# Attention backward: transposes of X ahead of the next block's first outputs, small row factors on Pool, one more empty slot in a background chain

## The chip, the cores and the metric

The kernel runs on one core of a Trainium2 chip. A core has TensorE (PE, matmuls), VectorE (DVE), ScalarE (ACT), GpSimd (Pool) and SyncE (SP, used here to issue DMAs). Each works through its own queue in order. The metric is device microseconds of one execution; a time before and a time after are medians over several runs. A profile is one execution, so its times are taken from that execution alone.

## The reference

The reference computes one block (attention of 32 heads with a head size of 16, an MLP with gelu, and a gate) and the gradients of its inputs. Sequence 2048, model size 512, MLP size 1792, all tensors in bf16:

```python
x = A_x
xn = _layernorm(x, axis=-1)
s = _A_ref(xn, A_wqkv, A_wo)            # softmax(q k^T / 4) v, then @ wo
g = _silu(_B_ref(xn, B_w1, B_b1, B_w2, B_b2))   # layernorm, gelu MLP
return x + s * g
```

The outputs are this value and its gradients with respect to A_x, A_wqkv, A_wo, B_w1, B_b1, B_w2 and B_b2 for a given grad_out (`jax.vjp`).

## The kernel before

Three stages follow each other. `phase_pre` makes the layer norms, q, k, v, the MLP's forward values and the gradient that enters the attention, and leaves them in DRAM. `attention_core` computes the attention forward and its gradients of q, k and v in one pass. `phase3` makes the remaining weight and input gradients. The change lies in `attention_core` alone, whose instruction order is written out by hand (`manual_schedule`): the order in which the Python code emits instructions is the order in each engine's queue.

Heads are handled in 16 pairs `p`, the 2048 queries in four chunks `qc` of 512. A pair and a chunk make a block, so there are 64 blocks `j`. A block has 16 steps, one for each key block `kb` of 128 keys; the global step number is `g`, with kb = g % 16. The pass is software-pipelined: while the steps of a block compute its exponentials and products, the Z matmuls of the block before it run three steps late (`lagb = 3`).

In each step:

- PE makes the scores `s` of the next step (`emit_s`, L696), the product `d` of the output gradient and the values for both heads (`emit_d`, L708), and in 10 of 16 steps the scores in the other orientation, `t` (`emit_t`, L682). The other six tiles of that kind come by DMA transpose.
- ACT takes the exponential of `s` into `eg` (`emit_exp_a`, L722) and of `t` into `e` (`emit_exp_b`, L730).
- DVE multiplies `d` by the exponential, once for each head (`emit_mult`, L740).
- PE accumulates X with the matmuls of the step before: `emit_l` (row sums, L766), `emit_e` (L778), `emit_g` (L790). X is one PSUM tile, so the next block's first `emit_l` must wait until X has been copied out.
- PE accumulates Z, the gradients of keys and values, of the block before (`emit_ze`, `emit_zg`, L856 and L868); after every four steps DVE adds Z to `acc` (`emit_acc`, L880 and L882).
- every fourth step SP issues a DMA transpose of `eg` into `tg` (`emit_dmat`, L751).

The scores share two PSUM buffers, and `d` shares two others with the transposed X (`ps_d`, tag "d"): a new `d` needs the product of the `d` before last to be done.

At the end of a block ACT copies X to `xs` (L795). In step 1 of the following block `emit_finalize` turns it into the outputs of 512 queries: four PE transposes of `xs` into XT (L805), a DVE copy to `xt` (L807), the reciprocal of the row sums `rL` (L817), the factors `dl` (L819) and `ndr` (L821), all 128x8. Pool then makes the weights W1 and W2 of the Z matmuls (L811, L822 to L824) and writes the attention output and the gradient of q (L826 to L833). The first Z matmul of a block that needs the new W1 is emitted at the end of step 3. In the order before, `emit_l`, `emit_e` and `emit_g` of step 0 stand ahead of the transposes in PE's queue.

Pool has three other tasks. At the start of a pair's second chunk and later (`load_ops`, `late`) it issues the loads of the next pair (L583 to L585) and copies them into a padded tile (L588, L589, and L596, L597 at step 13). When the last chunk of a pair has been accumulated it adds the two halves of `acc` (`hi`, `ob`, L888 and L889) and issues four DMAs of the result (L894); the last of this falls into steps 2 to 4 of the second chunk of the next pair, where the padding copies at step 5 follow. And a generator, `gelu_slope_ops`, computes the slope of the gelu for 56 tiles in the background. One of its slots is used at the end of each step, except at the steps kb = 2 and 3 and where `emit_finalize` runs (kb = 1), so a block has 13 slots. One iteration takes 12 slots: eleven hold Pool instructions (L631 and L632, loads L621, the store L657), one is empty. One of the slots also puts a Tanh into ACT's queue (L639), whose input `v` Pool makes in the slot before, and whose result Pool uses two slots later.

Of the kernel before, what the change touches and what calls it, by code (L numbers as in the profile page):

```python
# [9 lines left out]
f32 = mybir.dt.float32  # L10
ACT = mybir.ActivationFunctionType
ALU = mybir.AluOpType
# [529 lines left out]
def attention_core(ctx, tc, NAT_s, NATQ_s, Oall, dQall, dKVT_out, ident_f32, H1T_s, GP_s, npairs=16, nqc=4):  # L542
    nc = tc.nc
# [14 lines left out]
    finp = sb("finp", 2)  # L558
# [4 lines left out]
    for i in range(2):  # L563
# [4 lines left out]
            NATQq=opnd.tile([128, 16, 2, 17], bf16, name=f"NATQq{i}"),  # L568
            NATQd=opnd.tile([128, 16, 2, 16], bf16, name=f"NATQd{i}"),
# [34 lines left out]
    blocks = [(p, qc) for p in range(npairs) for qc in range(nqc)]  # L604
    NB = len(blocks)
    NSTEP = NB * 16
    st_s, st_t, st_d, st_et, st_e = {}, {}, {}, {}, {}
    blk = [dict(Gk={}, Ek={}) for _ in range(NB)]
# [8 lines left out]
    def gelu_slope_ops():  # L617
        def load(i):
            sc, fc = divmod(i, FC)
            x = bgp.tile([128, 512], bf16, name="bg_x")  # L620
            nc.gpsimd.dma_start(out=x[:], in_=H1T_s[fc * 128:(fc + 1) * 128, sc * 512:(sc + 1) * 512])  # L621
            return x
        nx = load(0)
        yield
        for i in range(n_slope):
            sc, fc = divmod(i, FC)
            x = nx
            m = bgp.tile([128, 512], bf16, name="bg_m")
            v = bgp.tile([128, 512], f32, name="bg_v", bufs=1)
            t = bgp.tile([128, 512], f32, name="bg_t", bufs=1)  # L630
            ts = lambda out, in_, a, b: nc.gpsimd.tensor_scalar(out=out[:], in0=in_[:], scalar1=a, scalar2=b, op0=ALU.mult, op1=ALU.add)  # L631
            tt = lambda out, a, b, op=ALU.mult: nc.gpsimd.tensor_tensor(out=out[:], in0=a[:], in1=b[:], op=op)  # L632
            tt(m, x, x)
            yield
            ts(v, m, GA, 1.0)
            yield
            tt(v, v, x)
            yield
            nc.scalar.activation(out=t[:], in_=v[:], func=ACT.Tanh, scale=GC)  # L639
            ts(m, m, 1.5 * GA * GC, 0.5 * GC)  # L640
            yield
            tt(m, m, x)
            if i + 1 < n_slope:
                nx = load(i + 1)
            yield
            tt(v, t, t)
            yield
            ts(v, v, -1.0, 1.0)
            yield
            tt(m, m, v)  # L650
            yield
            ts(t, t, 0.5, 0.5)
            yield
            tt(m, m, t, ALU.add)
            yield
            yield
            nc.gpsimd.dma_start(out=GP_s[fc * 128:(fc + 1) * 128, sc * 512:(sc + 1) * 512], in_=m[:])  # L657
            yield
    bg = gelu_slope_ops()

    def a_unit(g):
        return (g // 16, g % 16) if 0 <= g < NSTEP else None
# [5 lines left out]
    def op_of(j):  # L668
        return OP[blocks[j][0] % 2]
# [15 lines left out]
    def emit_s(g):  # L685
        a = a_unit(g)
        if a is None:
            return
        j, kb = a
        op = op_of(j)  # L690
        qc = blocks[j][1]
        s = ps_st.tile([128, 2, 512], f32, name="s", tag="st")
        st_s[g] = s
        for hj in range(2):
            r = 32 * hj
            nc.tensor.matmul(s[:, hj, :], lhsT=op["KVT"][r:r + 32, kb * 128:(kb + 1) * 128], rhs=op["QDT"][r:r + 32, qc * 512:(qc + 1) * 512],  # L696
                             start=True, stop=True, tile_position=(r, 0))
# [27 lines left out]
    def emit_exp_b(g):  # L725
        if g not in st_t:
            return
        e = ep.tile([128, 2, 512], bf16, name="e")
        st_e[g] = e
        nc.scalar.activation(out=e[:], in_=st_t.pop(g)[:], func=ACT.Exp)  # L730
# [12 lines left out]
    def emit_dmat(g):  # L743
        a = a_unit(g)
        if a is None or a[1] % 4 != 3:
            return
        j, kb = a
        kc = kb // 4
        n = n_moved[kc]
        tg = tgp.tile([128, 48, 128], bf16, name="tg")  # L750
        nc.sync.dma_start_transpose(out=tg[:, 0:8 * n + 32, :], in_=st_et[g][0][:, (4 - n) * 1024:8192])  # L751
        for i in range(n):
            blk[j]["Ek"][(kc, 4 - n + i)] = tg[:, 8 * i:8 * i + 8]
        blk[j]["Gk"][kc] = tg[:, 8 * n:8 * n + 32]
# [40 lines left out]
            nc.scalar.copy(out=xs[:], in_=X[:])  # L795
            blk[j]["xs"] = xs

    def emit_finalize(j):
        p, qc = blocks[j]
        NQq = op_of(j)["NATQq"]  # L800
        NQd = op_of(j)["NATQd"]
        xs = blk[j].pop("xs")
        XT = ps_d.tile([128, 4, 128], f32, name="XT", tag="d")
        for qb in range(4):
            nc.tensor.transpose(XT[:, qb, :], xs[:, qb * 128:(qb + 1) * 128], ident_f32[:])  # L805
        xt = finp.tile([128, 4, 128], f32, name="xt", bufs=1)
        nc.vector.tensor_copy(out=xt[:], in_=XT[:])  # L807
        XTv = xt[:].rearrange("q b (r c) -> q b r c", r=4)
        W1 = wp.tile([128, 4, 2, 32], bf16, name="W1")
        W2 = wp.tile([128, 4, 2, 32], bf16, name="W2")  # L810
        nc.gpsimd.memset(W2[:, :, :, 0:16], 0.0)  # L811
        st0 = qc * 4
        nqs = NQq[:, st0:st0 + 4, :, 1:17]
        ndo = NQd[:, st0:st0 + 4, :, :]
        bc = lambda ap: ap.to_broadcast([128, 4, 2, 16])
        rL = finp.tile([128, 4, 2, 1], f32, name="rL")
        nc.vector.reciprocal(out=rL[:], in_=XTv[:, :, 2:4, 17:18])  # L817
        dl = finp.tile([128, 4, 2, 1], f32, name="dl")
        nc.vector.tensor_tensor(out=dl[:], in0=XTv[:, :, 2:4, 0:1], in1=rL[:], op=ALU.mult)  # L819
        ndr = finp.tile([128, 4, 2, 1], f32, name="ndr")  # L820
        nc.vector.scalar_tensor_tensor(out=ndr[:], in0=dl[:], scalar=-1.0, in1=rL[:], op0=ALU.mult, op1=ALU.mult)  # L821
        nc.gpsimd.tensor_tensor(out=W1[:, :, :, 0:16], in0=ndo, in1=bc(rL[:]), op=ALU.mult)  # L822
        nc.gpsimd.tensor_tensor(out=W2[:, :, :, 16:32], in0=nqs, in1=bc(rL[:]), op=ALU.mult)
        nc.gpsimd.tensor_tensor(out=W1[:, :, :, 16:32], in0=nqs, in1=bc(ndr[:]), op=ALU.mult)  # L824
        Ov = Oall[:, st0:st0 + 4, p * 32:(p + 1) * 32].rearrange("q b (h c) -> q b h c", h=2)
        nc.gpsimd.tensor_tensor(out=Ov, in0=XTv[:, :, 0:2, 16:32], in1=bc(rL[:]), op=ALU.mult)  # L826
        t1 = finp.tile([128, 4, 2, 16], f32, name="t1")
        nc.gpsimd.tensor_tensor(out=t1[:], in0=XTv[:, :, 0:2, 0:16], in1=bc(dl[:]), op=ALU.mult)
        nc.gpsimd.tensor_tensor(out=t1[:], in0=XTv[:, :, 2:4, 1:17], in1=t1[:], op=ALU.subtract)
        rL4 = finp.tile([128, 4, 2, 1], f32, name="rL4")  # L830
        nc.gpsimd.tensor_scalar(out=rL4[:], in0=rL[:], scalar1=0.25, scalar2=None, op0=ALU.mult)
        dQv = dQall[:, st0:st0 + 4, p * 32:(p + 1) * 32].rearrange("q b (h c) -> q b h c", h=2)
        nc.gpsimd.tensor_tensor(out=dQv, in0=t1[:], in1=bc(rL4[:]), op=ALU.mult)  # L833
        blk[j]["W1"] = W1
        blk[j]["W2"] = W2
# [67 lines left out]
    for g in range(NSTEP + 16 + lagb):  # L903
        a = a_unit(g)
        if a is not None:
            j, kb = a
            p, qc = blocks[j]
            if kb == 0 and qc == 1 and p + 1 < npairs:
                for i, f in enumerate(load_ops(p + 1)):
                    late.append((g + 1 + 4 * i, f))  # L910
        for it in [x for x in late if x[0] <= g]:
            late.remove(it)
            it[1]()
        first = g % 16 == 1
        gz = g - lagb
        i = gz % 4
        emit_s(g + 1)
        emit_d(g, 0)
        if not first:
            emit_l(g - 1)  # L920
        if i == 0:
            emit_e(g - 1)
        else:
            emit_ze(gz)
            if i % 2 == 1:
                emit_zg(gz - 1)
                emit_zg(gz)
        emit_d(g, 1)
        emit_t(g)
        emit_exp_a(g + 1)  # L930
        emit_exp_b(g)
        emit_mult(g)
        emit_acc(gz)
        emit_dmat(g)
        if first:
            emit_l(g - 1)
        if i != 0:
            emit_e(g - 1)
        emit_g(g - 1)
        if i == 0:  # L940
            emit_ze(gz)
        if g >= 17 and (g - 17) % 16 == 0 and (g - 17) // 16 < NB:
            emit_finalize((g - 17) // 16)
        elif g % 16 not in (2, 3):
            next(bg, None)
    for it in late:
# [108 lines left out]
```

## Time and profile before

| | |
|---|---|
| Median of 4 runs | 2495.18 us (2484.98 to 2521.93) |
| The profiled execution | 2490.88 us |
| Its span, first to last instruction | 2488.9 us |
| Mean granted TensorE clock | 0.951 |
| First and last copy of X (L795) | 328.4 and 2071.6 us |
| PE products of `d` (L708) | 2048, 392 ns each |
| ACT exponentials of `s` (L722) and `t` (L730) | 1024 of 1034 ns, 640 of 1036 ns |
| DVE products (L740) | 2048, 686 ns each |
| DVE waiting for XT at L807 | 60.0 us, 64 times |
| ACT waiting for Pool before the Tanh (L639) | 11.1 us, 4 times |

How to read it: the attention stage takes some 1780 us of the span. A row of the page gives a group's busy time and the mean of one instruction; instructions of one engine overlap a little at their ends, so starts that follow each other are closer than the durations say (exponentials that run back to back start 0.92 us apart). The idle time behind the second bar is that of the engine just before the group, with the engine whose instruction ended it.

### The profile page before, as it was taken

How to read it: one execution, taken by the hardware profiler on the slowest of the kernel's cores; microseconds unless marked ns; L12 is line 12 of the kernel's file. 1: busy time of each engine (PE TensorE's matmuls, PEld its weight loads, DVE VectorE, ACT ScalarE, POOL GpSimd, SP SyncE). 2: the span in 40 equal slices, each digit the busy share in tenths (PEclk: the TensorE clock that was granted, in tenths of full speed). 3: DMA queues.
4: the chain of work that ended last, by engine and by line, in shares of the span. 5: the costliest groups of instructions: out<-in, count | busy, mean ns of one | idle time of the engine just before them, and what ended most of it. 6: DMA issues, size and time to landing. Idle time of an engine off the chain costs nothing.

```text
span 2488.9 us, 47595 instructions
## 1 busy us (share of the span) xinstructions
PE 2231.0 (90%) x18408; PEld 757.4 (30%) x18448; DVE 1843.3 (74%) x3222; ACT 1815.5 (73%) x2102; POOL 1113.3 (45%) x1678
## 2 busy tenths in 40 slices
PE   3688599999999999999999999999999997589997
PEld 2233122222222222222222222222222222234446
DVE  5665388898889888888888988888889883112652
ACT  3354289999899999899898999989999994011241
POOL 0533454666557476665657575664313121110020
PEclk8799689999999999999899999999999998789999
DMA  5355499999999999999999999999999998997565
GB/s 192 99 185 180 110 225 224 251 235 241 218 246 239 237 245 239 229 229 247 222 232 230 235 233 223 254 227 233 224 232 232 231 217 202 260 231 204 150 125 125
DMA packets 1743125, 534.88 MB, mean 215 GB/s; under 512 B 1664433, under 2 KB 1721906, under 8 KB 1742898
## 3 DMA queue, kind: packets, MB, share of 16 engines
q1 hardware_dynamic: 1671554, 449.37, 89.0%
q10 hardware_dynamic: 61104, 54.93, 7.2%
q0 software_dynamic: 10240, 27.54, 3.8%
q8 instruction: 144, 2.36, 0.4%
q14 instruction: 83, 0.68, 0.1%
HBM read 52.83 MB, written 62.66 MB: 46 GB/s over the span
## 4 chain that ended last, share of the span: by engine, by line
PE 51%; ACT 18%; DMA 11%; DVE 8%; POOL 6%; issue 4%; SPq 2%; ACTq 1%; DVEq 0%; POOLq 0%
PE d L708 10%; PE X L766 9%; ACT e L730 8%; PE s L696 8%; ACT eg L722 7%; PE X L778 4%; DMA tg<-eg 4%; PE X L790 3%; PE Z L868 3%; PE ps_dhg L465 2%; DVE eg L740 2%; PE Z L856 2%; DMA hgc<-HGT_s 1%; PE ps_h L212 1%; DMA hgc<-DH1T_s 1%
## 5 line engine op out<-in xcount | busy, mean ns | idle before, releaser
L740 DVE TENSOR_TENSOR eg<-d,eg 128x512 bf16<-128x512 f32 x2048 | 1340.6, 686 | 182.8 <-PE d L708 71.4
L722 ACT ACTIVATE eg<-s 128x1024 bf16<-128x1024 f32 x1024 | 1042.4, 1034 | 96.7 <-PE s L696 43.2
L708 PE MATMUL d<-QDT,KVT 32*128 32x512 bf16 x2048 | 800.9, 392 | 14.3 <-DVE eg L740 14.0
L730 ACT ACTIVATE e<-t 128x1024 bf16<-128x1024 f32 x640 | 663.0, 1036 | 47.9 <-PE t L682 46.1
L696 PE MATMUL s<-QDT,KVT 32*128 32x512 bf16 x2048 | 408.0, 393 | 72.4 <-ACT eg L722 54.2
L766 PE MATMUL X<-eg,Lc 128*32 128x512 bf16 x2048 | 412.0, 399 | 5.3
L778 PE MATMUL X<-eg,NAT 128*32 128x512 bf16 x2048 | 411.7, 399 | 0.0
L790 PE MATMUL X<-eg,NAT 128*17 128x512 bf16 x2048 | 406.0, 393 | 0.0
L708 PEld LDWEIGHTS <-KVT 32*128 32x128 bf16 x2048 | 186.9, 91 | 342.4 <-issue 342.4
L856 PE MATMUL Z<-e,W 128*32 128x512 bf16 x1280 | 255.9, 395 | 4.7 <-POOL W L824 3.8
L682 PE MATMUL t<-KVT,QDT 32*128 32x512 bf16 x1280 | 254.6, 392 | 5.4 <-ACT eg L722 5.2
L822 POOL TENSOR_TENSOR W<-NATQd,rL 128x128 bf16<-128x128 bf16 x64 | 25.8, 402 | 468.6 <-DVE rL L817 468.6
L696 PEld LDWEIGHTS <-KVT 32*128 32x128 bf16 x2048 | 116.0, 91 | 307.1 <-issue 307.0
L868 PE MATMUL Z<-tg,W 128*32 128x512 bf16 x2048 | 208.5, 388 | 0.0
L766 PEld LDWEIGHTS <-Lc 128*32 128x32 bf16 x2048 | 104.4, 93 | 329.0 <-issue 324.9
L856 PE MATMUL Z<-tg,W 128*32 128x512 bf16 x768 | 154.3, 398 | 0.0
L778 PEld LDWEIGHTS <-NAT 128*32 128x32 bf16 x2048 | 99.4, 94 | 165.1 <-issue 165.1
L882 DVE TENSOR_TENSOR acc<-Z,acc 128x512 f32<-128x512 f32 x192 | 130.5, 680 | 13.1 <-PE Z L868 13.1
L856 PEld LDWEIGHTS <-W 128*32 128x32 bf16 x2048 | 113.5, 93 | 38.7 <-issue 24.9
L270 POOL TENSOR_TENSOR dx<-lnb_prod,lnb_dy 128x512 bf16<-128x512 f32 x16 | 20.3, 1266 | 214.0 <-DMA dout<-in_grad_out_dram 184.4
L790 PEld LDWEIGHTS <-NAT 128*17 128x17 bf16 x2048 | 93.5, 88 | 59.5 <-issue 59.5
L632 POOL TENSOR_TENSOR bg_v<-bg_t 128x512 f32<-128x512 f32 x56 | 58.4, 1043 | 80.0 <-ACT bg_t L639 79.3
(167 smaller groups left out, 2729.5 us busy)
## 6 DMA issues: line engine op xcount, KB each, us to landing
HGT_s<-hgT SPq DMA_DIRECT2D x2, 3584.0 KB, 12.4
bg_x<-H1T_s POOLq DMA_DIRECT2D x56, 128.0 KB, 5.4
GP_s<-bg_m POOLq DMA_DIRECT2D x56, 128.0 KB, 5.4
gp<-GP_s ACTq DMA_DIRECT2D x8, 896.0 KB, 6.9
DH1T_s<-dh1T SPq DMA_DIRECT2D x4, 1792.0 KB, 10.3
NAT<-NAT_s POOLq DMA_DIRECT2D x16, 264.0 KB, 6.0
GB_s<-gB ACTq DMA_DIRECT2D x16, 256.0 KB, 2.0
tg<-eg SPq DMA_TRANSPOSE x256, 8.6
```

The lines of the kernel that those rows point to most:

```text
L682: nc.tensor.matmul(t[:, hj, :], lhsT=op["QDT"][r:r + 32, q0:q0 + 128], rhs=op["KVT"][r:r + 32, kc * 512:(kc + 1) * 512], start=True, stop= ...
L696: nc.tensor.matmul(s[:, hj, :], lhsT=op["KVT"][r:r + 32, kb * 128:(kb + 1) * 128], rhs=op["QDT"][r:r + 32, qc * 512:(qc + 1) * 512], start ...
L708: nc.tensor.matmul(d[:], lhsT=op["KVT"][r:r + 32, kb * 128:(kb + 1) * 128], rhs=op["QDT"][r:r + 32, qc * 512:(qc + 1) * 512], start=True, ...
L722: nc.scalar.activation(out=cur["eg"][1][:, :, kb % 4, :, :].rearrange("k b h q -> k h b q"), in_=st_s.pop(g)[:].rearrange("k h (b q) -> k ...
L730: nc.scalar.activation(out=e[:], in_=st_t.pop(g)[:], func=ACT.Exp)
L740: nc.vector.tensor_tensor(out=gts[:, kb % 4, hj, :].rearrange("k (b q) -> k b q", b=4), in0=ds[hj][:].rearrange("k (b q) -> k b q", b=4), ...
L766: nc.tensor.matmul(X[64 + 32 * hj:96 + 32 * hj, :], lhsT=Lc[:], rhs=et[:, :, kb % 4, hj, :], start=(kb == 0), stop=False, skip_group_check ...
L778: nc.tensor.matmul(X[32 * hj:32 * hj + 32, :], lhsT=NATt[:, kb, hj, 1:33], rhs=et[:, :, kb % 4, hj, :], start=(kb == 0), stop=(kb == 15), ...
L790: nc.tensor.matmul(X[64 + 32 * hj:64 + 32 * hj + 17, :], lhsT=NATt[:, kb, hj, 0:17], rhs=gts[:, kb % 4, hj, :], start=False, stop=(kb == 1 ...
L856: nc.tensor.matmul(Z[32 * hj:32 * hj + 32, :], lhsT=blk[j]["W1"][:, qb, hj, :], rhs=ev[:, hj], start=(i == 0), stop=False, tile_position=( ...
L868: nc.tensor.matmul(Z[c:c + 32, :], lhsT=blk[j]["W2"][:, qb, hj, :], rhs=gv[:, :, hj, qb, :], start=(i == 1), stop=(i >= 2), tile_position= ...
L882: nc.vector.tensor_tensor(out=av, in0=Z[:], in1=av, op=ALU.add)
```

## The change

The transposes of X, their copy and the reciprocal move from `emit_finalize` into a new `emit_xt`, which is emitted ahead of `emit_l`, `emit_e` and `emit_g` in the same step. `dl` and `ndr` go from DVE to Pool; `ndr` becomes two Pool instructions, and both halves of W1 now stand ahead of W2. The generator gets one more empty slot between the slot that makes `v` and the one that issues the Tanh, so that an iteration takes 13 slots.

```diff
             tt(v, v, x)
             yield
+            yield
             nc.scalar.activation(out=t[:], in_=v[:], func=ACT.Tanh, scale=GC)
             ts(m, m, 1.5 * GA * GC, 0.5 * GC)
...
-    def emit_finalize(j):
-        p, qc = blocks[j]
-        NQq = op_of(j)["NATQq"]
-        NQd = op_of(j)["NATQd"]
+    def emit_xt(j):
         xs = blk[j].pop("xs")
         XT = ps_d.tile([128, 4, 128], f32, name="XT", tag="d")
         for qb in range(4):
             nc.tensor.transpose(XT[:, qb, :], xs[:, qb * 128:(qb + 1) * 128], ident_f32[:])
         xt = finp.tile([128, 4, 128], f32, name="xt", bufs=1)
         nc.vector.tensor_copy(out=xt[:], in_=XT[:])
+        XTv = xt[:].rearrange("q b (r c) -> q b r c", r=4)
+        rL = finp.tile([128, 4, 2, 1], f32, name="rL")
+        nc.vector.reciprocal(out=rL[:], in_=XTv[:, :, 2:4, 17:18])
+        blk[j]["xt"] = (xt, rL)
+
+    def emit_finalize(j):
+        p, qc = blocks[j]
+        NQq = op_of(j)["NATQq"]
+        NQd = op_of(j)["NATQd"]
+        xt, rL = blk[j].pop("xt")
...
-        rL = finp.tile([128, 4, 2, 1], f32, name="rL")
-        nc.vector.reciprocal(out=rL[:], in_=XTv[:, :, 2:4, 17:18])
+        nc.gpsimd.tensor_tensor(out=W1[:, :, :, 0:16], in0=ndo, in1=bc(rL[:]), op=ALU.mult)
         dl = finp.tile([128, 4, 2, 1], f32, name="dl")
-        nc.vector.tensor_tensor(out=dl[:], in0=XTv[:, :, 2:4, 0:1], in1=rL[:], op=ALU.mult)
+        nc.gpsimd.tensor_tensor(out=dl[:], in0=XTv[:, :, 2:4, 0:1], in1=rL[:], op=ALU.mult)
         ndr = finp.tile([128, 4, 2, 1], f32, name="ndr")
-        nc.vector.scalar_tensor_tensor(out=ndr[:], in0=dl[:], scalar=-1.0, in1=rL[:], op0=ALU.mult, op1=ALU.mult)
-        nc.gpsimd.tensor_tensor(out=W1[:, :, :, 0:16], in0=ndo, in1=bc(rL[:]), op=ALU.mult)
+        nc.gpsimd.tensor_scalar(out=ndr[:], in0=dl[:], scalar1=-1.0, scalar2=None, op0=ALU.mult)
+        nc.gpsimd.tensor_tensor(out=ndr[:], in0=ndr[:], in1=rL[:], op=ALU.mult)
+        nc.gpsimd.tensor_tensor(out=W1[:, :, :, 16:32], in0=nqs, in1=bc(ndr[:]), op=ALU.mult)
         nc.gpsimd.tensor_tensor(out=W2[:, :, :, 16:32], in0=nqs, in1=bc(rL[:]), op=ALU.mult)
-        nc.gpsimd.tensor_tensor(out=W1[:, :, :, 16:32], in0=nqs, in1=bc(ndr[:]), op=ALU.mult)
...
         emit_dmat(g)
+        fin = (g - 17) // 16 if first and 0 <= (g - 17) // 16 < NB else None
+        if fin is not None:
+            emit_xt(fin)
         if first:
             emit_l(g - 1)
...
-        if g >= 17 and (g - 17) % 16 == 0 and (g - 17) // 16 < NB:
-            emit_finalize((g - 17) // 16)
+        if fin is not None:
+            emit_finalize(fin)
```

## The prediction

> **What bounds the kernel now.** I read the page first (busy shares, the clock row), then the busy time of a long stretch of the attention stage, then the order of time around one block change, and last the waits on the tanh. The profiled execution took 2490.88 us with a span of 2488.9 us; the median of the four runs shown is 2495.18 us, 4.3 us above it. All sums below are made against the 2490.88 us.
>
> ```profile
> PE 2231.0 (90%) x18408; PEld 757.4 (30%) x18448; DVE 1843.3 (74%) x3222; ACT 1815.5 (73%) x2102; POOL 1113.3 (45%) x1678
> ...
> PEclk8799689999999999999899999999999998789999
> 332.00:2072.00 1740.00, 1659.58 (x15595) 492.91 (x15593) 1525.39 (x2514) 1610.52 (x1752) 955.35 (x1506) 0.98 1.16 234
> ```
>
> Between 332 and 2072 us PE is busy for 95%, ACT for 93%, DVE for 88%, Pool for 55% of the time. No engine is saturated alone; what counts is which hand-over comes late. 1740 us hold 63 blocks, 27.6 us each. The order of time around one block change (start, duration, engine, line; in brackets the idle time before and what ended it):
>
> ```profile
> 1019.98 0.58 ACT L795 COPY xs<-X 128x512 f32<-128x512 f32 x1
> 1020.61 0.39 PE L766 MATMUL X<-eg,Lc 128*32 128x512 bf16 x2
> 1021.15 0.66 PE L805 MATMUL XT<-ident_f,xs 128*128 128x128 f32 x4
> 1021.91 0.69 DVE L807 COPY xt<-XT 128x512 f32<-128x512 f32 x1 [0.91 <-PE XT L805]
> 1023.27 1.27 DVE L740 TENSOR_TENSOR eg<-d,eg 128x512 bf16<-128x512 f32 x2
> 1024.00 0.37 PE L708 MATMUL d<-QDT,KVT 32*128 32x512 bf16 x1 [0.24 <-DVE eg L740]
> 1025.95 1.02 ACT L722 ACTIVATE eg<-s 128x1024 bf16<-128x1024 f32 x1 [0.80 <-PE s L696]
> ```
>
> X is copied by 1020.56 (I call that base). PE first does the six matmuls of emit_l, emit_e and emit_g, then the transposes; DVE idles 0.91 us for them, copies, makes three small factors, and starts its next product at base+2.71. PE's next d needs the PSUM buffer which that product frees and starts at 1024.00, although its partner s started at 1023.37; elsewhere the two start within 0.01 us. That 0.6 us reaches ACT as 0.80 us of idleness.
>
> The second loss is rare and large:
>
> ```profile
> 996.63 2.02 POOL L894 DMA_DIRECT2D dKVT_s<-ob  x4 [0.29 <-POOL ob L889]
> 998.66 1.16 POOL L632 TENSOR_TENSOR bg_v<-bg_v,bg_x 128x512 f32<-128x512 f32 x1
> ...
> 999.86 0.63 ACT L639 ACTIVATE bg_t<-bg_v 128x512 f32<-128x512 f32 x1 [2.76 <-POOL bg_v L632]
> ...
> 1001.45 0.39 PE L696 MATMUL s<-QDT,KVT 32*128 32x512 bf16 x2 [3.29 <-ACT eg L722]
> ```
>
> ```profile
> 988.54:1020.55 32.01, 28.39 (x248) 7.64 (x248) 24.41 (x41) 26.25 (x30) 23.31 (x38) 0.89 1.10 232
> 1102.17:1129.09 26.92, 25.59 (x248) 7.75 (x248) 24.45 (x41) 25.52 (x29) 21.64 (x36) 1.00 1.25 257
> 1326.51:1359.14 32.63, 29.01 (x250) 7.68 (x248) 24.59 (x40) 26.22 (x29) 22.90 (x37) 0.84 1.11 234
> ```
>
> ACT stands in its queue behind a tanh whose input Pool has not finished, PE runs dry, and its granted clock falls to a mean of 0.84 to 0.89 over the block. The tile bg_t shows four such waits, 11.1 us in all. Each makes a block of 32.0 to 33.0 us from one of 26.9 to 27.2: some 5.5 us.
>
> [...] gaps of 3.29 us and even 1.67 us are followed by half clock here. [...] an instruction that waits holds those behind it, as the tanh above does. [...] 128x8 takes 0.234 us (L831), 128x128 0.40 us.
>
> **The change, part by part.**
>
> *Transposes forward.* They need xs (base) and the buffer of d whose product ended 0.15 us before base, so they can start at base+0.05 instead of 0.59. They hold PE 0.59 us (to the next matmul), so the six matmuls follow at 0.64 and the next s at 1.18, as now: PE's order changes, not its sum. DVE copies from 0.81 to 1.50 (the lag of 0.10 behind the transposes and 0.69 as now). No DMA issue moves with it.
>
> *Two factors leave DVE, the reciprocal stays.* rL ends at 1.73; dl (0.17) and ndr (0.27) no longer follow on DVE. The next product starts at 1.77 instead of 2.71 and ends at 2.46. s of that step must still wait for an exp of ACT and starts at 2.81 as now; its d follows at once instead of at 3.44: 0.62 us won. The next d but one waits for DVE too and comes 0.76 us earlier (DVE's chain moves from 3.31 to 2.55 there, where it meets the d at 2.09). I take 0.65 us, 64 times: -41.6 us. Bounds: 0, if another wait steps in; 0.94 us, all that DVE gains, -60 us.
>
> *Pool's chain.* Before the last W1 half stand now dl, the two steps of ndr, instead of W2. No row shows a 128x8 product on Pool. Low end 0.17 us each (the 128x512 and 128x128 products, 1.1 and 0.40 us, carried down to 8 elements); high end 0.40 us, the 128x128 row. I take 0.25 with hand-over, 0.75 us together. W1 is done at about 1.83 + 0.36 + 0.75 + 0.40 = 3.3; the first Z matmul that needs it comes at base+4.63 now, 4.0 then. Hidden with 0.7 us to spare; if the cover goes, each 0.1 us costs PE 0.1 us. With the high end W1 is done at 3.8, still in time.
>
> *The extra yield.* An iteration of the background slope now takes 13 slots, and a block has 13 (16 steps less 1, 2 and 3). So each iteration sits at the same place of every block, where 12 slots let it drift: v is finished at step 5, the tanh comes after the exps of step 7. In blocks of the first query chunk that follow a finished pair (13 while the background runs) Pool has, in program order: load of the next pair, finalize, hi/ob, four dKVT issues, v's first half, two Pad copies, v's second half. From base: the last slope product before it ends 0.17; three issues 1.7 -> 1.9; finalize 3.2 + 0.75 -> 5.85; hi, ob and issues 4.33 (as from 994.32 to 998.65) -> 10.2; 0.62 -> 10.8; Pad copies 1.2 -> 12.0; product 1.16 and hand-over -> 13.2. ACT has done the exp before the tanh at base+11.3 in the undisturbed block above; 0.65 earlier makes 10.7. So ACT waits 2.5 us in all 13, where it waits 2.76 us in 4 now. Costs scale from 5.5 us: 5.2. Nine more are +47 us, four a little shorter -1 us. Behind the tanh stand the exps, and behind these PE's s and DVE's products. The yield adds no work.
>
> *Other blocks.* After a tanh at this place no block lost time before (26.8 us). Blocks behind a standstill are shorter (27.13 us against 28.56 and 28.60 for two others), since the DMA transposes catch up: for nine more about -6 us after deducting seams that wait for DMA anyway.
>
> Sum: -41.6 + 47 - 1 - 6 = -1.6 us, 2489 us for the profiled execution; between that and the median's offset I say 2490.
>
> **The rivals.**
>
> *A, the standstills vanish.* If v is ready by base+10.7 in the pair blocks, the seams gain 42 us and the four waits' 22 us go: 2491 - 42 - 22 = 2427. For it: a tanh one slot later is exactly more time for Pool. Against: 2.5 us are missing and Pool's list has no gap.
>
> *B, the new Pool chain holds PE up (the slower side).* Place: the first Z matmul of each block, waiting for W1. Price: whatever W1 passes base+4.0 by. It decides from three small operations of 0.47 us each; at 0.7 us each all 0.65 us of a seam are gone. Then only the standstills' +47 - 6 remain: 2532. For it: Pool waited for here already (W, 3.8 us on PE). Against: 0.234 us for the like-sized L831.
>
> *C, the transposes do not come forward.* The profile puts 0.43 us of the wait before them down to DVE; if they need the second product (base+0.44) they hold the six matmuls, DVE gains only its 0.44 us, PE loses that much: seam gain nil, 2532. Against: in the profile they start 0.32 us behind the matmul ahead of them, PE's usual pace, and in some blocks before that product has ended.
>
> **Chances.** Likeliest case 0.66 (its own range 2462 to 2521: 0.4 to 0.9 us per seam, 4.6 to 6.3 us per standstill), A 0.13, B 0.13, C 0.08. The range 2450 to 2536 holds the first and B and C, and leaves A out. Faster by over 1% (below 2470; about what a measurement of this kernel can tell from no change): 0.13 + 0.05 = 0.18. Slower (above 2520): 0.21 of which some falls short, plus the first case's edge: 0.20. Within: 0.62.
>
> **What will show it.** In the profile after: DVE's wait for XT falls from 0.94 to about 0.4 us a block; the d behind s at a block change starts with it; ordinary blocks are 26.2 us. bg_t has 13 waits for Pool of about 2.5 us, 32 us in all, 108 us apart, each followed by half clock. No new wait of Z for W. The prediction is wrong if the waits on bg_t are few or short (then A), if Z waits for W in most blocks (B), or if half clock follows less often than 13 times.

## The result, and the profile after

| | before | after |
|---|---|---|
| Median of all runs | 2503.95 us (61 runs, 2481.78 to 2535.66) | 2525.77 us (38 runs, 2483.64 to 2551.24) |
| Ratio of comparable runs | 1 | 1.0023, interval 1.0000 to 1.0047 |
| The profiled execution | 2490.88 us | 2545.43 us |
| Its span and mean granted clock | 2488.9 us, 0.951 | 2543.7 us, 0.897 |

The change makes the kernel slower by about 0.2%, at the edge of what can be told from nothing. Comparable runs are those within 1.5% of their kernel's fastest; the medians of all runs differ by 0.9%, and the profile after is of a run outside that limit. The forecast was 2490 us against 2495.18 us, so 0.2% faster: the time lies in the range, the sign is wrong. The two profiled executions are 55 us apart, much more than the medians: before's is 13 us better than its median, after's 20 us worse. The granted clock goes with the time of an execution: the fastest of after, 2483.64 us, had a mean of 0.927, the slowest, 2551.24 us, one of 0.898.

From the profile of after, the busy times, the clock row (tenths of full speed, 40 slices) and ACT's row of the exponentials; then the same row of before:

```profile
PE 2289.9 (90%) x18408; PEld 750.1 (29%) x18448; DVE 1830.7 (72%) x3094; ACT 1821.2 (72%) x2102; POOL 1155.0 (45%) x1870
PEclk8799669898989989898898989898998998799998
L723 ACT ACTIVATE eg<-s 128x1024 bf16<-128x1024 f32 x1024 | 1045.2, 1034 | 93.8 <-PE d L709 81.5 <-DMA tg<-eg 5.7 <-DVE eg L741 1.6
L722 ACT ACTIVATE eg<-s 128x1024 bf16<-128x1024 f32 x1024 | 1042.4, 1034 | 96.7 <-PE s L696 43.2 <-PE d L708 36.5 <-DMA tg<-eg 8.5
```

The work is the same, but PE is busy for 59 us longer, since its clock falls again and again. The clock records of all kernels here show two values, full clock (1.0) and half clock (0.5). In the attention stage nearly every second slice is an 8 where before had 9. ACT's wait for `s`, 43.2 us in the profile before, no longer shows in its row; its wait for `d` has grown from 36.5 to 81.5 us.

The order of time around a block change of after (start, duration, engine, line; X has been copied at 534.28):

```profile
533.70 0.58 ACT L796 COPY xs<-X 128x512 f32<-128x512 f32 x1
534.63 0.63 PE L803 MATMUL XT<-ident_f,xs 128*128 128x128 f32 x4 [0.38 <-DVE eg L741]
535.19 0.39 PE L767 MATMUL X<-eg,Lc 128*32 128x512 bf16 x2
535.36 0.69 DVE L805 COPY xt<-XT 128x512 f32<-128x512 f32 x1 [0.28 <-PE XT L803]
535.73 0.39 PE L697 MATMUL s<-QDT,KVT 32*128 32x512 bf16 x2
535.73 0.39 PE L709 MATMUL d<-QDT,KVT 32*128 32x512 bf16 x1
536.16 1.02 ACT L723 ACTIVATE eg<-s 128x1024 bf16<-128x1024 f32 x1
536.26 1.45 DVE L741 TENSOR_TENSOR eg<-d,eg 128x512 bf16<-128x512 f32 x2
```

`s` and `d` start together and ACT no longer idles there: its 0.80 us are won, and a block without trouble takes 25.98 us instead of 26.80. Now the other side: who waited for XT, and for the tanh's input, in all of after (engine that was waited for; us and times):

```profile
  PE XT L803: 26.6, 63
```

```profile
  POOL bg_v L632: 33.0, 13
```

DVE waits 0.42 us a block for XT. The tanh waits 13 times, 33.0 us. All stand in the second block of a pair, called a pair block below. One of them, in the block that begins at 445.8, in order of time:

```profile
453.94 2.04 POOL L901 DMA_DIRECT2D dKVT_s<-ob  x4 [0.29 <-POOL ob L896]
456.06 0.61 POOL L631 TENSOR_SCALAR bg_v<-bg_m 128x512 f32<-128x512 bf16 x1
456.72 0.67 POOL L588 COPY Pad<-NAT 128x544 bf16<-128x544 bf16 x1
457.33 0.60 POOL L589 COPY Pad<-NAT 128x512 bf16<-128x512 bf16 x1
457.91 1.15 POOL L632 TENSOR_TENSOR bg_v<-bg_v,bg_x 128x512 f32<-128x512 f32 x1
459.08 0.63 ACT L640 ACTIVATE bg_t<-bg_v 128x512 f32<-128x512 f32 x1 [2.08 <-POOL bg_v L632]
460.68 0.61 PE L697 MATMUL s<-QDT,KVT 32*128 32x512 bf16 x2 [2.90 <-ACT eg L723]
```

Pool's list ends at base + 13.3, as foretold. The exponential behind the tanh in ACT's queue starts at 459.62, 0.54 us after the tanh, and PE stands for 2.90 us. From then on the matmuls of `s` take 0.61 us instead of 0.39. Busy times of this block, the next and the one after it (window, length, then PE, PEld, DVE, ACT and Pool busy with counts, granted clock, DMA share, GB/s):

```profile
445.80:480.90 35.10, 32.13 (x248) 7.46 (x248) 23.95 (x38) 26.39 (x29) 22.16 (x39) 0.70 1.15 226
480.90:508.30 27.40, 26.96 (x253) 8.00 (x251) 24.53 (x40) 25.71 (x30) 13.97 (x24) 0.95 1.05 226
508.30:534.30 26.00, 25.42 (x248) 7.66 (x248) 23.62 (x38) 25.54 (x30) 13.97 (x24) 1.00 1.05 235
```

A gap of 2.90 us makes a block 9.1 us longer, and the half clock runs into the next block too. In an undisturbed block ACT and PE are busy for 98% of the time: no slack is left to catch up in.

Between copies of X, blocks 2 to 62 take 1689.8 us in the profile before and 1726.2 us after, 36.4 us more. This sum is made up as follows: 61 blocks at 0.82 us less, -50.0 us; what lies above the undisturbed length grows from 55.0 us (before, over 26.80) to 141.4 us (after, over 25.98). Of the 141.4 us, 112.3 are in the 13 blocks with a tanh wait, 7.2 in block 57, 19.1 in the blocks behind these. The other 18 us of the two spans' difference are 11.8 us in the first block, which ran at half clock throughout, and the rest outside.

### The profile page after: what moved, and what is told of

It is laid out like the page before. It is cut to its first block, busy times and chain, and to the rows that moved or that the text cites. A ratio compares the mean times of both kernels' runs of the same rounds, so it can differ in the third digit from the quotient of the medians.

```text
span 2543.7 us, 47712 instructions
## 1 busy us (share of the span) xinstructions
PE 2289.9 (90%) x18408; PEld 750.1 (29%) x18448; DVE 1830.7 (72%) x3094; ACT 1821.2 (72%) x2102; POOL 1155.0 (45%) x1870
## 4 chain that ended last, share of the span: by engine, by line
PE 53%; ACT 17%; POOL 10%; DMA 9%; DVE 5%; issue 4%; SPq 1%; ACTq 1%; POOLq 0%; DVEq 0%
PE d L709 10%; PE s L697 10%; PE X L767 10%; ACT eg L723 8%; ACT e L731 7%; PE X L779 6%; PE Z L875 3%; PE X L791 3%; PE ps_dhg L465 2%; DMA hgc<-DH1T_s 2%; PE ps_dy L480 1%; PE ps_h L212 1%; DMA hgc<-HGT_s 1%; POOL ob L896 1%; PE ps_dw L530 1%
## 5 line engine op out<-in xcount | busy, mean ns | idle before, releaser
L741 DVE TENSOR_TENSOR eg<-d,eg 128x512 bf16<-128x512 f32 x2048 | 1354.5, 688 | 279.7 <-PE d L709 125.8
L723 ACT ACTIVATE eg<-s 128x1024 bf16<-128x1024 f32 x1024 | 1045.2, 1034 | 93.8 <-PE d L709 81.5
L709 PE MATMUL d<-QDT,KVT 32*128 32x512 bf16 x2048 | 848.3, 415 | 0.1
L697 PE MATMUL s<-QDT,KVT 32*128 32x512 bf16 x2048 | 430.5, 415 | 82.0 <-ACT eg L723 62.0
L767 PE MATMUL X<-eg,Lc 128*32 128x512 bf16 x2048 | 435.4, 422 | 0.0
L779 PE MATMUL X<-eg,NAT 128*32 128x512 bf16 x2048 | 435.0, 422 | 0.0
L791 PE MATMUL X<-eg,NAT 128*17 128x512 bf16 x2048 | 427.7, 415 | 0.0
L863 PE MATMUL Z<-e,W 128*32 128x512 bf16 x1280 | 269.1, 416 | 3.4 <-POOL W L830 2.0
L683 PE MATMUL t<-KVT,QDT 32*128 32x512 bf16 x1280 | 267.8, 413 | 2.0 <-ACT eg L723 2.0
L875 PE MATMUL Z<-tg,W 128*32 128x512 bf16 x2048 | 219.0, 412 | 0.0
L863 PE MATMUL Z<-tg,W 128*32 128x512 bf16 x768 | 161.8, 418 | 0.0
```

Source lines behind the costliest of these rows:

```text
L683: nc.tensor.matmul(t[:, hj, :], lhsT=op["QDT"][r:r + 32, q0:q0 + 128], rhs=op["KVT"][r:r + 32, kc * 512:(kc + 1) * 512], start=True, stop= ...
L709: nc.tensor.matmul(d[:], lhsT=op["KVT"][r:r + 32, kb * 128:(kb + 1) * 128], rhs=op["QDT"][r:r + 32, qc * 512:(qc + 1) * 512], start=True, ...
L723: nc.scalar.activation(out=cur["eg"][1][:, :, kb % 4, :, :].rearrange("k b h q -> k h b q"), in_=st_s.pop(g)[:].rearrange("k h (b q) -> k ...
L741: nc.vector.tensor_tensor(out=gts[:, kb % 4, hj, :].rearrange("k (b q) -> k b q", b=4), in0=ds[hj][:].rearrange("k (b q) -> k b q", b=4), ...
L767: nc.tensor.matmul(X[64 + 32 * hj:96 + 32 * hj, :], lhsT=Lc[:], rhs=et[:, :, kb % 4, hj, :], start=(kb == 0), stop=False, skip_group_check ...
L779: nc.tensor.matmul(X[32 * hj:32 * hj + 32, :], lhsT=NATt[:, kb, hj, 1:33], rhs=et[:, :, kb % 4, hj, :], start=(kb == 0), stop=(kb == 15), ...
```

## The experiments

Ratios are to the kernel before, run on the same chip, with a 95% interval. "12 slots" is the generator of before, "13 slots" that of after. First the parts of the change by themselves: is it the extra slot that costs?

**no_yield**: after with 12 slots.

```diff
             tt(v, v, x)
             yield
-            yield
```

> The changed kernel without the extra empty slot (12 slots an iteration, as before). Theory M (block changes gain 0.8 us each; the standstills behind the tanh, multiplied by the 13-slot iteration, take it back): ordinary blocks stay at 26.0 us, the waits of the tanh fall from 13 to 4, each longer than the 2.76 us of before (about 4 us, since ACT comes 0.8 us earlier and Pool 0.75 us later); 45 us faster than before, ratio 0.980 to 0.985. Rival W (the block change or Pool's longer chain is what costs): ratio 0.995 or more, and half clock for over 150 us in the attention stage as in the changed kernel.

Measured 1.0055 (1.0028 to 1.0082): no gain at all, where four waits and a ratio of 0.980 to 0.985 had been expected. Undisturbed blocks took 25.98 us as in after, but 8 tanh waits were left (22.9 us), five of them of 4.1 us, and in other pairs Z stood for W. Block 29 of this kernel, Pool and then PE in order of time:

```profile
1121.23 0.22 POOL L818 MEMSET W<- 128x128 bf16 x1
1122.38 0.21 POOL L828 TENSOR_TENSOR ndr<-ndr,rL 128x8 f32<-128x8 f32 x1
1122.67 0.40 POOL L829 TENSOR_TENSOR W<-NATQq,ndr 128x128 bf16<-128x128 bf16 x1
...
1123.12 0.39 PE L862 MATMUL Z<-e,W 128*32 128x512 bf16 x2 [1.35 <-POOL W L829]
```

Pool comes to `emit_finalize` with background work and three load issues ahead of it. So where the slots drift, Pool's lateness appears as one wait or the other. Taking the extra slot out is no cure.

**yield_only**: before with 13 slots.

```diff
             tt(v, v, x)
             yield
+            yield
```

> The kernel before with the extra empty slot alone. M: ordinary blocks 26.8 us as before; the tanh waits in all 13 pair blocks, but shorter than in the changed kernel, about 1.1 us (Pool is done with v at base+12.4 without the three small operations, ACT at base+11.3); if such short waits still cool the clock, 20 to 70 us slower, ratio 1.008 to 1.03. Rival W: the slot is harmless, ratio 0.990 to 1.000, because four long waits are exchanged for 13 short ones.

Measured 1.0149 (1.0066 to 1.0232): the slot alone makes before slower. 13 tanh waits, 17.0 us in all. Two blocks with the same wait (1.53 us) and the same PE gap (1.65 us), busy times as above:

```profile
903.70:932.10 28.40, 26.06 (x248) 7.80 (x248) 24.18 (x41) 25.62 (x29) 21.03 (x35) 1.00 1.24 252
1012.50:1047.30 34.80, 32.84 (x248) 7.58 (x247) 24.39 (x40) 26.44 (x30) 21.65 (x36) 0.71 1.13 228
```

The same gap cost 1.6 us in one block and 8 us in the other (over 26.80). The difference is the clock: PE does the same work in 26.06 and in 32.84 us.

**xt_only**: before with the transposes of X forward, `dl` and `ndr` still on DVE, 12 slots.

```diff
         emit_dmat(g)
+        if fin is not None:
+            emit_xt(fin)
         if first:
             emit_l(g - 1)
```

> 12 slots as before; the transposes moved ahead as in the change, but dl and ndr left on DVE and W1, W2 made in the old order on Pool. Theory P (the block change gains, and Pool's list at the start of a pair, longer by three operations and asked for earlier, gives it back as one gap of PE and half clock in each pair block): ordinary blocks 26.2 to 26.4 us, since DVE keeps its 0.44 us; waits of Z for W in pair blocks gone or under 0.7 us; the tanh waits about 3.3 us in 4 blocks; ratio 0.985 to 1.000, better than the 1.0055 of the changed kernel with 12 slots. Rival T (the order of the transposes is what disturbs): ratio 1.005 or more.

Measured 0.9991 (0.9967 to 1.0016). Undisturbed blocks took 26.26 us, 0.54 us less than before. Seven tanh waits, 14.6 us in all, against four and 11.1 us before: all gain is given back.

**pool_only**: before with `dl` and `ndr` on Pool, transposes where they were, 12 slots.

```diff
-        nc.vector.tensor_tensor(out=dl[:], in0=XTv[:, :, 2:4, 0:1], in1=rL[:], op=ALU.mult)
+        nc.gpsimd.tensor_tensor(out=dl[:], in0=XTv[:, :, 2:4, 0:1], in1=rL[:], op=ALU.mult)
...
-        nc.vector.scalar_tensor_tensor(out=ndr[:], in0=dl[:], scalar=-1.0, in1=rL[:], op0=ALU.mult, op1=ALU.mult)
+        nc.gpsimd.tensor_scalar(out=ndr[:], in0=dl[:], scalar1=-1.0, scalar2=None, op0=ALU.mult)
+        nc.gpsimd.tensor_tensor(out=ndr[:], in0=ndr[:], in1=rL[:], op=ALU.mult)
```

> 12 slots as before; the transposes stay behind emit_l, emit_e and emit_g, dl and ndr go to Pool in the changed order. P: ordinary blocks 26.4 to 26.8 us; Z waits for W by over 1 us in a third of the pair blocks (those where Pool issues the loads late), tanh waits of about 3.5 us in 4; ratio 1.000 to 1.015. Rival T: as before, 0.998 to 1.002, because Pool's small operations are hidden.

Measured 1.0080 (1.0041 to 1.0120), with undisturbed blocks of 26.26 us too. Z waited for W in five blocks of a pair's second chunk, in four by 1.3 us and in one by 2.95; the tanh waited seven times, 18.6 us. Each of the three edits alone brings nothing or a loss, although two of them shorten the block. (The two gains of 0.54 us are not to be added: together they make 0.82.)

Then the wait itself: what if the tanh doesn't wait?

**nowait**: after, but the tanh reads the loaded `x` instead of `v`, so the slope of the gelu that it leads to is another function.

```diff
-            nc.scalar.activation(out=t[:], in_=v[:], func=ACT.Tanh, scale=GC)
+            nc.scalar.activation(out=t[:], in_=x[:], func=ACT.Tanh, scale=GC)
```

> The changed kernel, but the tanh takes the loaded tile x in place of v (the gelu's slope is left wrong), so that ACT has nothing to wait for; every instruction and its place stay. It prices the 13 waits by themselves. P: no wait on bg_t, pair blocks of 26 to 28 us instead of 35; 60 to 90 us less than the changed kernel, ratio to before 0.970 to 0.988; what stays of half clock comes from waits for the DMA transposes in the third quarter of a pair. Rival D (other waits take their place: Z for W, exps for the DMA): ratio 0.995 or more.

Measured 0.9947 (0.9919 to 0.9976), near the rival. No tanh wait is left, and blocks of the second chunk have a median of 26.50 us instead of 34.96. But the next blocks now take 29.34 us. One of the new waits, SP's queue and ACT in order of time:

```profile
767.40 27.66 SPq L752 DMA_TRANSPOSE tg<-eg  x4
795.12 5.34 SPq L592 DMA_TRANSPOSE KVT<-Pad  x1
800.56 12.40 SPq L752 DMA_TRANSPOSE tg<-eg  x2
...
800.86 1.94 ACT L723 ACTIVATE eg<-s 128x1024 bf16<-128x1024 f32 x2 [2.49 <-DMA tg<-eg]
```

SP works without a pause, one transpose after the other, and the transposes of the next pair's operands stand among those of `eg`. An exponential may overwrite its `eg` buffer only when that has been transposed, so ACT waits. Over the kernel these waits grow from 5.7 us (after) to 24.7 us. The standstill had hidden them.

**tanh8**: 13 slots, but both empty slots ahead of the tanh, which comes a step later.

```diff
             tt(v, v, x)
             yield
             yield
+            yield
             nc.scalar.activation(out=t[:], in_=v[:], func=ACT.Tanh, scale=GC)
...
-            yield
```

> The changed kernel with the second empty slot moved too from the end of the iteration to ahead of the tanh, which then comes after the exps of step 8. M: 13 waits as in the changed kernel, of about 0.9 instead of 2.5 us, since ACT gets there 1.7 us later; PE gaps of about 1.4 us; half clock in some of the pair blocks only; ratio 0.975 to 0.995. Rival W: any of these waits costs the same 9 us, since the clock and not the wait is paid: ratio 1.00.

Measured 1.0107 (1.0038 to 1.0176), slower than either theory expected. Two things add up. Undisturbed blocks took 26.44 us, 0.46 us more than in after, some 28 us in 61 blocks; why is not shown. And the pair blocks cost hardly less than in after, 102.6 us above the undisturbed length instead of 112.3, though the waits were short: in all 13 Z waited 0.93 to 0.95 us for W. In five of them half clock followed that wait, and the tanh then had none. In the other eight it did not, but later the tanh waited 0.84 to 0.95 us, PE stood for 1.66 to 1.77 us, and half clock followed that. What such a wait did at 446.13, PE's matmul and then the busy times from 437 to 471:

```profile
446.13 0.39 PE L863 MATMUL Z<-e,W 128*32 128x512 bf16 x2 [0.95 <-POOL W L830]
```

```profile
437.00:471.00 34.00, 32.92 (x238) 7.20 (x234) 23.57 (x37) 25.31 (x28) 26.46 (x43) 0.65 1.17 243
```

0.95 us of idleness, then by the clock record half clock from 447.1 to 481.2, of which the window shows the first 24 us. So shorter waits did not spare the clock. In each of the 14 traces the recorded changes of the clock (43 in before, 63 in after) lie whole multiples of 3.41 us apart, to 0.01 us; the times a whole number of these steps away from them are called the grid here, each one a grid line. From the records, gaps of nearly equal length by the time from the grid line before them to their start; the 13 of tanh8 are the waits of Z for W, all at the same place of the program:

```
tanh8, gaps of 0.93 to 0.95 us
  starting 1.51 1.57 1.75 1.75 1.93 us behind a grid line            half clock 34.1 us, each time
  starting 0.24 0.46 0.48 0.48 0.48 0.59 2.52 3.06 us behind it      none, each time
yield_only, gaps of 1.65 to 1.68 us
  starting 0.88  1.20  1.62  1.62  1.72  1.81  1.83  2.21 us behind it
  half clock 13.7  23.9  3.4   3.4   20.5  23.9  23.9  none (us)
```

This separates gap length from cost: the 13 gaps of tanh8 have one length and one place in the program, and the five differ from the eight in where they began in the grid. No full rule follows from it. In yield_only the place does not tell how long half clock lasts. In clean_dve below one gap of 0.72 us, 2.14 us behind a line, was followed by 23.9 us of half clock, while seven of 0.70 to 0.72 us, at 0.42 to 0.58 or 2.73 to 2.92 us, were followed by none.

Next, a cure for Pool's list by timing alone.

**phase10**: after, with the slots turned so that `v` is made at steps 10 to 12 of a block and the tanh comes at step 15.

```diff
+        for _ in range(7):
+            yield
...
             tt(v, v, x)
             yield
             yield
+            yield
...
-            yield
```

> The changed kernel with 13 slots, but the iteration shifted within the block: v is made at steps 10 to 12, both empty slots stand behind it, the tanh comes after the exps of step 15, and seven empty slots go ahead of the first iteration. M: no wait of the tanh at all, blocks of 26.0 us for all query chunks but those held by DMA, little half clock behind the first block; 75 us faster than before, ratio 0.965 to 0.975. Rival W: half clock and blocks of 33 to 35 us stay in the pair blocks without a tanh wait, ratio 0.99 or more.

Measured 0.9898 (0.9822 to 0.9974), between the two. The tanh waits are gone (one of 0.3 us) and second blocks take 26.38 us, but third blocks have a median of 29.17. A second and a third block (busy times), and ACT and SP in the third:

```profile
771.10:797.50 26.40, 25.52 (x248) 7.68 (x248) 24.04 (x39) 25.51 (x30) 21.77 (x38) 1.00 1.24 253
797.50:829.80 32.30, 29.13 (x248) 7.80 (x248) 23.76 (x38) 25.80 (x29) 15.42 (x27) 0.84 1.20 230
```

```profile
805.56 1.75 SPq L600 DMA_TRANSPOSE QDT<-Pad  x1
807.41 26.10 SPq L754 DMA_TRANSPOSE tg<-eg  x4
...
817.21 1.94 ACT L725 ACTIVATE eg<-s 128x1024 bf16<-128x1024 f32 x2 [2.99 <-DMA tg<-eg]
```

The same wait as in nowait: SP's queue works without a pause, and has two more transposes to take in.

**spread**: phase10, with the copy and the transpose of the next pair's queries 16 steps later, so that the two extra transposes are a block apart.

```diff
-                    late.append((g + 1 + 4 * i, f))
+                    late.append((g + 1 + 4 * i + (16 if i >= 3 else 0), f))
```

> The shifted iteration of the earlier run (v made at steps 10 to 12, tanh at step 15), and the copy and the DMA transpose of the next pair's queries put off by 16 steps, into the next block. In the earlier run SP's queue ran without a break from the second to the third block of a pair, and the exps waited for it. P: third blocks fall from a median of 29.2 to under 27 us, half clock to less than 40 us behind the first block; ratio 0.970 to 0.982. Rival C (the clock falls in these blocks without the DMA): third blocks stay above 28.5 us, ratio 0.988 or more.

Measured 2432.67 us, 0.9677 (0.9640 to 0.9714), beyond what was expected. Two blocks at the same place, busy times:

```profile
762.20:788.60 26.40, 25.52 (x248) 7.69 (x248) 24.02 (x39) 25.50 (x30) 21.94 (x38) 1.00 1.26 253
788.60:815.00 26.40, 25.42 (x248) 7.62 (x248) 24.03 (x39) 25.68 (x30) 15.23 (x26) 1.00 1.24 253
```

Half clock in the attention stage falls from 126 us (phase10) to 30 us behind the first block, and the exponentials' waits for transposes from 23.9 to 9.4 us.

Is that the change's merit, or the cures'? Four kernels have the cures without the change, with a part of it, or one cure alone.

**clean_before**: before with both cures (slots turned, later query transposes), and no edit at the block change.

> The kernel before with the two cures of the fastest run so far (iteration shifted to steps 10 to 15, query transposes of the next pair 16 steps later), but none of the change at the block change. It prices that part alone, with nothing around it that can take the gain back. Theory Q (the block change gains 0.82 us in every block, and lost it only to Pool's list and the DMA queue): ordinary blocks 26.8 us, ratio to before 0.984 to 0.992, so 50 us above the 0.968 of the run with the change. Rival E (the cures make the whole gain, the block change little): ratio 0.965 to 0.975.

Measured 2455.07 us, 0.9763 (0.9701 to 0.9826), between the two expectations and nearer to the rival: the cures alone give 2.4%, most of the gain. Behind the first block the clock record shows half clock in two blocks only. ACT's row in this kernel:

```profile
L725 ACT ACTIVATE eg<-s 128x1024 bf16<-128x1024 f32 x1024 | 1044.7, 1035 | 82.7 <-PE s L699 45.7 <-PE d L711 26.4 <-DMA tg<-eg 3.7
```

and in spread:

```profile
L725 ACT ACTIVATE eg<-s 128x1024 bf16<-128x1024 f32 x1024 | 1043.4, 1035 | 58.2 <-PE d L711 40.5 <-DMA tg<-eg 9.4 <-DVE eg L743 2.0
```

The 45.7 us that ACT waits for `s`, the 0.7 us of each block change, are what the edit removes. Blocks 2 to 62 take 1646.6 us in clean_before and 1614.4 us in spread: 32.2 us, 0.53 us a block. The medians differ by 22.4 us, 0.9%. The intervals of the two ratios just touch (0.9701 and 0.9714); of four runs each, the slowest of spread (2435.58 us) is still faster than the fastest of clean_before (2437.06 us).

**clean_dve**: spread with `dl` and `ndr` back on DVE, directly behind the reciprocal; the diff is that of pool_only the other way round.

> The same two cures with the transposes moved ahead, but dl and ndr on DVE and the old order of W1 and W2. Q: ordinary blocks 26.3 us, as in the 12-slot run with these factors on DVE, so that the factors are worth 0.3 us a block or 19 us and the transposes 0.5 us or 32 us; ratio 0.972 to 0.980. Rival E: 0.965 to 0.970, the same as with the factors on Pool.

Measured 2429.11 us, 0.9671 (0.9597 to 0.9745), no different from spread. An undisturbed block takes 26.26 us instead of 25.97, and blocks 2 to 62 take 1622.8 us instead of 1614.4, while Z's waits for W fall from 6.0 to 1.4 us. The medians don't tell the two apart, so the move of the factors to Pool is not shown to be worth anything in the whole kernel; the transposes forward are what pays: against clean_before, blocks 2 to 62 take 23.7 us less.

**after_spread** and **before_spread**: after and before with the later query transposes only, as in the diff of spread.

> The changed kernel with the later query transposes alone; the 13 waits of the tanh stay. It prices them where the DMA queue cannot take their place. Q: 13 waits of about 2.5 us on bg_t, pair blocks of 33 to 35 us, third and fourth blocks 26 to 27 us; ratio 0.995 to 1.005, that is 70 to 90 us above the run with both cures. Rival F (the DMA queue alone was what gave the gain back): ratio 0.970 to 0.985.

Measured 1.0033 (0.9991 to 1.0075): nothing. The tanh waits are there, 12 by this profile (28.5 us), and second blocks have a median of 34.15 us; only the blocks behind them shrink, to 26.10 us.

> The kernel before with the later query transposes alone. Q: before had the DMA queue's slack, so third blocks fall only from 27.7 to 26.9 us; the four tanh waits stay; ratio 0.990 to 0.998. Rival E: ratio under 0.985, the DMA queue was a bound before too.

Measured 0.9949 (0.9919 to 0.9979): half a per cent. So neither cure does it alone: turned slots without later transposes give 1.0%, later transposes without turned slots 0.5% on before and nothing on after, both together with the block change 3.2%.

## Why the prediction was wrong, point by point

**Right: the block change.** The forecast took 0.65 us a block (bounds 0 and 0.94). An undisturbed block won 0.82 us, all of ACT's 0.80 us; with both cures in place the edit is worth 0.53 us averaged over all blocks. Its path was a little different: the transposes started at base + 0.35, not + 0.05, since in the shorter block the product whose `d` buffer they need ends later (rival C's mechanism, at a third of a microsecond). It did no harm: ACT's exponential of `t` ran until 536.1, when that `s` was done.

**Right: Pool's chain in ordinary blocks.** The three small operations take 0.20 to 0.23 us and follow each other at 0.31 us, 0.9 us together; Z waits for W once in the whole of after, for 2.0 us, behind the last block. The 0.7 us to spare do not hold where `emit_finalize` comes late in Pool's queue, in the second block of a pair; in after the locked slots keep background work out of its way, in no_yield they don't.

**Right: 13 waits.** They came where foretold (a pair's second blocks, which the prediction calls those of the first chunk), 33.0 us against 32, 1.8 to 5.2 and on average 2.5 us each, and half clock followed all 13.

**Wrong: "Costs scale from 5.5 us: 5.2".** This is the step that failed. The four standstills before left 7 to 10 us of half clock each, and their cost was taken for a property of the wait. In after the half clock that followed lasted 7 to 24 us, mostly 20 to 24, and a pair block took 34.96 us in the median: 9.0 us above the undisturbed length, 8.6 on average, not 5.2. With 8.6 us the forecast's own sum is -41.6 + 13 x 8.6 - 4 x 5.5 - 6, or some 42 us slower. In yield_only the same gap cost 1.6 or 8 us. So a standstill's price is mostly the clock's, and not in proportion to its length: the gaps of after (2.6 to 2.9 us, one of 5.6) were shorter than before's 3.29 us but for one.

What differed is where half clock ended. Before, it ended in all four cases 21 to 23 us into the same block. In after it began somewhat later in the block (13.6 to 16.4 us behind the copy of X, against 11.1 to 14.1), and in 10 of 13 cases it outlasted the block and ended 2.0 to 5.1 us into the next. Whether before's four were lucky or typical of their place is not shown; in before_spread, with the same four standstills, three ended within the block (7 to 10 us) and one lasted 27.3 us. What makes both kernels' times spread so widely is not shown either.

**Wrong: "Other blocks", -6 us.** Blocks behind a standstill were to be shorter, as SP catches up. SP did, and waits for the transposes fell (8.5 to 5.7 us), but the half clock ran 2 to 5 us into ten of the 13: 27.25 us in the median against 25.98, some 18 us over 13 blocks.

**The sum.** -50 us at the block changes instead of -41.6; blocks with a tanh wait 112 us above the undisturbed length instead of 13 times 5.2, 68 us; the blocks behind +19 instead of shorter. In the profiled executions that makes 36 us more in blocks 2 to 62; by the medians of comparable runs some 6 us (0.0023 times 2504), by those of all runs 22 us. The size of the miss in a typical execution is therefore smaller than one profile makes it look. The term is the same: in after_spread, whose profiled execution (2513.36 us) lies close to its median, the 13 pair blocks stand 101 us above the undisturbed length, against 68 us in the forecast.

**The rivals.** A (no standstills, 2427 us) did not happen, but its price was right by chance: spread, where they are cured, takes 2432.67 us; by nowait, removing the tanh wait alone would have given only 2502.00, as the transposes come up next. B did not happen in after; in pool_only it did, in pair blocks. C held back 0.3 us and nothing more.

**Open.** Half clock lasted 3.4 us in some cases (two of yield_only) and 23.9 to 34.1 us in others (after, tanh8), with PE at work throughout. The clock records show where it tends to end: of 77 stretches of half clock in the 14 traces that were still on 2 us behind a copy of X, 71 ended at the first grid line to come. What in these steps brings the full clock back, no run here settles. Places of the tanh other than steps 7, 8 and 15, and those by which it drifts with 12 slots, were not tried.

## What to carry to other kernels

A gain of a fraction of a microsecond on the critical path is only worth what the next hand-overs allow: here two of the three edits shortened the block, and Pool's list at a pair's start and SP's transpose queue took it back. Before an edit to a background chain's period, work out whether it locks to the loop, and at which step it then meets the engine's longest list: the same 13 slots turned by seven steps made a loss of 0.2% into a gain of 1.0%, and with the transposes spread 3.2%. Price a stall of PE by the clock that follows, as a range and not as one number, and look up in the clock record where half clock ended: in tanh8 a stall of 0.95 us early in a block was followed by 34.1 us of it.

## What the runs showed of the hardware

A PE gap of 0.94 us was followed by 34.1 us of half clock five times out of five when it began 1.5 to 1.9 us behind a line of the 3.41 us grid, and by none in the eight cases that began elsewhere in the grid (tanh8). Half clock lasted whole multiples of 3.41 us, from 3.4 to 44.4 us behind the first block (the longest in before_spread), and 71 of the 77 stretches still on 2 us behind a copy of X ended at the next grid line. Three dependent 128x8 operations on Pool took 0.20 to 0.23 us each and started 0.31 us apart (medians, after). SP took 4.8 to 8.7 us for one transpose of `eg` (median 5.9, after); four of them fill 23.7 of a block's 26 us, and each of the next pair's two others took 1.4 to 4.9 us (after).
